# Moving the pool of converted weights and g by 64 bytes in a fused attention and MLP kernel

## The chip, the cores and the metric

The kernel runs on one core of one Trainium2 chip. The metric is the time of one execution in microseconds (us), and lower is better. Before the change the median of three runs is 1013.45 us (1012.03 to 1017.72).

## What is computed

Random-feature attention over 8 batches, 8 heads, 576 positions and a head size of 64, then an MLP with an ELU over the 4608 tokens of width 512, with 2048 hidden units:

```python
q_s, k_s = q * scale, k * scale                       # phi(x) = exp(h - max(h)) / sqrt(m),
q_p, k_p = phi(q_s), phi(k_s)                         # h = x @ omega.T - |x|^2 / 2
kv = einsum('bhsm,bhsd->bhmd', k_p, v); z = sum(k_p, axis=2)
attn = einsum('bhsm,bhmd->bhsd', q_p, kv) / (einsum('bhsm,bhm->bhs', q_p, z)[..., None] + 1e-06)
x = attn.transpose(0, 2, 1, 3).reshape(4608, 512)
h = x @ w_in                                          # 4608 x 2048
g = where(h > 0, h, exp(min(h, 0)) - 1)
out = g @ w_out                                       # 4608 x 512
```

## The kernel before

**Tiling.** The 4608 tokens are cut into 12 blocks of 384 (`TB`). The hidden units are cut into 16 slices of 128 (`NF`). One step of the MLP is one slice for one block, so there are 192 steps. The first three blocks are gone through twice with 8 slices each, the other nine once with 16 slices.

**Precision by halves.** Each MLP operand is held as a high part, in a reduced form that TensorE reads in one pass, and a low part that holds what is left. The weights of the first layer are `w1c` (high at `[:, 0]`, low at `[:, 1]`), the input is `xh` and `xl`, the second layer's weights are `w2h` and `w2l`, and the activation is `g` (high and low). Each product is three matmuls: high by high, high by low, low by high.

**Layer 1** (`layer1`, L1014 to L1016). For each of four chunks `c` of the width, three matmuls of 384 columns. The stationary operand, which is loaded into the array ahead of the matmul, is a 128x128 slice of `w1c`. The moving operand, which is streamed through, is `xh` or `xl`. That makes 12 matmuls a step, 2304 in all. Then ScalarE and VectorE make `g` from the result (L1023 to L1027, then the two halves of `g`).

**Layer 2** (`layer2`, L1052 to L1054). For each of three groups of 128 tokens, three matmuls of 512 columns: 9 a step, 1728 in all. The stationary operand is a 128x128 slice of `g`, and the moving operand is `w2h` (L1052, L1054) or `w2l` (L1053). While one matmul streams, TensorE loads the stationary operand of the next.

**Attention.** 32 pairs of heads are worked through beside the MLP. Their matmuls stand between those of the MLP: L566 (`om` streamed, `tk` or `tq` loaded), L776 (`zr` streamed, `ones` loaded), L732 (a transpose: `ident` streamed, a part `kvt` of a `zs` buffer loaded), and others. `visit` and `finish` hold these.

**Order.** A planner (`Plan`) gives each operation a due time and a cost and writes out the order of every engine ahead of time. It works from constants and does not look at addresses.

**Where things lie.** The bytes of a partition are given out in the order of the pools. The pool `const` comes first: `ident`, `ones`, `of`, `om`, two `kvf`, `w2h`, `w2l`, `xh`, `xl`. All of these have sizes that are multiples of 256 bytes, so they all start at the same place modulo 256. Then come the padding tile `gap0`, the pool `mv` (three `w1c` buffers of 4096 bytes, three `g` buffers of 3072 bytes) and the pool `sb`, which begins with the padding tile `gap1` and holds the rest. `sb` has, in this order, the tiles for loads (`xk`, `xq` and so on, 3 of 4608 bytes), the tiles `tk` and `tq` (2 of 4608), `v` (2, each taking 2624 bytes), two small ones of 512, the four buffers `raw` and `zs` (4608 apart), and then the smaller and later tiles.

The slices that the matmuls take move by multiples of 256 bytes too (512 bytes for a chunk of `w1c` or a token group of `g`, 1536 for a block of `xh`, 2048 for a slice of `w2h`). So each pair of a streamed and a loaded operand has one fixed distance modulo 256. The lines that set it:

```python
GAP = 48                                              # L33
    const.tile([P, GAP], F32, name="gap0")            # L391: 4 * GAP bytes
    sb.tile([P, 64 - GAP], F32, name="gap1")          # L392
```

Of the kernel before, what the change touches and what calls it, by code (L numbers as in the profile page):

```python
# [29 lines left out]
NTT = TB // P  # L30
NBLK = NTOK // TB
RING = 2 * S
GAP = 48  # L33
NJ = 9
NV = 10 * (D + 1)
SCALE = 1.0 / (float(D) ** 0.25)
# [303 lines left out]
def performer_elu_kernel(  # L340
# [49 lines left out]

    const.tile([P, GAP], F32, name="gap0")  # L391
    sb.tile([P, 64 - GAP], F32, name="gap1")  # L392

# [810 lines left out]
```

## Time and profile before

| | |
|---|---|
| median of three runs | 1013.45 us (1012.03, 1013.45, 1017.72) |
| profiled execution | 1011.99 us, span 1010.2 us |
| granted TensorE clock, mean | 0.999 |
| PE busy (matmul) | 995.6 us, 99% of the span, 5806 matmuls |
| PEld busy (weight load) | 883.0 us, 87% |
| DVE, ACT, POOL busy | 722.9, 656.2, 254.1 us (72%, 65%, 25%) |

Matmuls overlap in the pipeline and their ends are modelled, so the duration of one is longer than the distance between two starts. PE is TensorE's matmul, PEld its weight load, DVE is VectorE, ACT is ScalarE and POOL is GpSimd. A name such as `acc<-w2h,g` gives the output, the streamed operand and the loaded operand, in that order.

### The profile page before, as it was taken

What the parts mean: (1) busy time and instruction counts of PE and PEld (TensorE: products, weight loads), DVE (VectorE), ACT (ScalarE), POOL (GpSimd) and SP (SyncE); (2) the same over time, 40 slices, a digit from 0 to 9 for tenths busy, and PEclk for the clock granted to TensorE, in tenths of its full rate; (3) what the DMA queues carried; (4) which work ended last, traced back from release to release, by engine and by line L of the source; (5) the groups of instructions that cost most, each with busy time, mean ns of one, the idle gap of its engine ahead of it and who ended that gap; (6) DMA issues with size and microseconds to landing.
All of it is one profiled execution on the core that took longest, in us unless ns stands there. A gap on an engine that the chain in (4) does not pass through costs nothing. (4 is left out here: it accounts for less than half of the span.)

```text
span 1010.2 us, 18666 instructions
## 1 busy us (share of the span) xinstructions
PE 995.6 (99%) x5806; PEld 883.0 (87%) x5806; DVE 722.9 (72%) x2605; ACT 656.2 (65%) x1797; POOL 254.1 (25%) x273
## 2 busy tenths in 40 slices
PE   9899999999999999999999999999999999999998
PEld 8788889888888988999888988999888888899997
DVE  7999998559979974367888985448788886433332
ACT  7888744589869954268878983438888884322322
POOL 3666532333423320012322421003322241000000
PEclk9999999999999999999999999999999999999999
DMA  9577877467796875347666775435777644533431
GB/s 226 177 219 247 270 273 260 167 231 262 242 294 215 265 234 164 137 155 227 215 221 210 268 242 181 156 125 181 250 230 237 236 156 155 175 130 129 163 133 53
DMA packets 73779, 204.91 MB, mean 203 GB/s; under 512 B 10256, under 2 KB 22736, under 8 KB 73680
## 3 DMA queue, kind: packets, MB, share of 16 engines
q1 hardware_dynamic: 73680, 203.72, 61.7%
q8 instruction: 47, 0.77, 0.3%
q14 instruction: 52, 0.43, 0.1%
HBM read 169.35 MB, written 34.34 MB: 202 GB/s over the span
## 5 line engine op out<-in xcount | busy, mean ns | idle before, releaser
L1014 PE MATMUL ph<-xh,w1c 128*128 128x384 f32 x768 | 261.9, 341 | 1.0 <-DVE e L1027 1.0
L1015 PE MATMUL ph<-xl,w1c 128*128 128x384 f32 x768 | 258.3, 336 | 0.0
L1016 PE MATMUL ph<-xh,w1c 128*128 128x384 f32 x768 | 258.1, 336 | 0.0
L1023 ACT ACTIVATE e<-ph 128x384 f32<-128x384 f32 x192 | 95.0, 495 | 223.9 <-PE ph L1016 214.1
L1052 PE MATMUL acc<-w2h,g 128*128 128x512 f32 x576 | 228.1, 396 | 0.0
L1053 PE MATMUL acc<-w2l,g 128*128 128x512 f32 x576 | 227.0, 394 | 0.0
L1054 PE MATMUL acc<-w2h,g 128*128 128x512 f32 x576 | 224.6, 390 | 0.0
L1027 DVE SCALAR_TENSOR_TENSOR e<-e,ph 128x384 f32<-128x384 f32 x192 | 105.3, 550 | 164.3 <-ACT e L1024 162.9
L1014 PEld LDWEIGHTS ph<-xh,w1c 128*128 128x128 f32 x768 | 144.4, 188 | 19.9 <-DVE e L1027 2.3
L1015 PEld LDWEIGHTS ph<-xl,w1c 128*128 128x128 f32 x768 | 144.4, 188 | 12.9
L1016 PEld LDWEIGHTS ph<-xh,w1c 128*128 128x128 f32 x768 | 144.4, 188 | 0.0
L404 POOL TENSOR_TENSOR hq<-hq,den 128x512 f32<-128x512 f32 (+1 forms) x96 | 81.6, 862 | 228.0 <-DVE den L806 159.8
L1054 PEld LDWEIGHTS acc<-w2h,g 128*128 128x128 f32 x576 | 108.1, 188 | 24.3
L1052 PEld LDWEIGHTS acc<-w2h,g 128*128 128x128 f32 x576 | 108.3, 188 | 7.5 <-issue 1.3
L1053 PEld LDWEIGHTS acc<-w2l,g 128*128 128x128 f32 x576 | 108.3, 188 | 4.9 <-POOL w2l L404 0.3
L404 DVE TENSOR_TENSOR g<-e,g 128x384 fp32r<-128x384 f32 x176 | 103.6, 590 | 3.2
L1024 ACT ACTIVATE e<-e 128x384 f32<-128x384 f32 x192 | 101.5, 530 | 3.5
L659 POOL TENSOR_TENSOR zs<-hk 128x512 f32<-128x512 f32 x24 | 31.1, 1297 | 218.9 <-ACT hk L488 160.1
L797 DVE CUSTOM_DVE_ANT_0 junk<-hq,pz 128x128 f32<-128x128 f32 (+1 forms) x320 | 73.9, 279 | 6.5 <-PE pz L776 4.5
L575 ACT ACTIVATE p2k<-ppk,sqk 128x128 f32<-128x128 f32 x216 | 66.3, 369 | 18.4 <-PE ppk L566 12.1
L488 ACT ACTIVATE hk<-hk,mnk 128x128 f32<-128x128 f32 x216 | 68.9, 401 | 4.3 <-DVE mnk L584 4.2
L401 DVE CAST g<-e 128x384 fp32r<-128x384 f32 x168 | 64.5, 386 | 9.8 <-PE acc L1054 0.9
(184 smaller groups left out, 1472.8 us busy)
## 6 DMA issues: line engine op xcount, KB each, us to landing
w1c<-w1s SPq DMA_DIRECT2D x176, 512.0 KB, 3.5
raw_w<-in_w_dram SPq DMA_DIRECT2D x32, 512.0 KB, 4.9
xk<-in_kx_dram SPq DMA_DIRECT2D x24, 576.0 KB, 4.8
xq<-in_qx_dram SPq DMA_DIRECT2D x24, 576.0 KB, 4.4
turned<-tb SPq DMA_DIRECT2D x24, 576.0 KB, 3.0
qh<-turned SPq DMA_DIRECT2D x96, 144.0 KB, 4.8
v<-in_v_dram SPq DMA_DIRECT2D x32, 325.0 KB, 5.1
out_dram<-o SPq DMA_DIRECT2D x36, 256.0 KB, 4.1
```

The lines of the kernel that those rows point to most:

```text
L404: (nc.vector if e == "DVE" else nc.gpsimd).tensor_tensor(*args)
L488: nc.scalar.activation(h()[:, j, :], src(j), AF.Exp, bias=mn()[:, j:j + 1], scale=-1.0)
L797: nc.vector.tensor_tensor_reduce(out=junk()[r], in0=h()[r, j, :], in1=pz()[r, a * P:(a + 1) * P], scale=1.0, scalar=EPS, op0=ALU.mult, op1 ...
L1014: nc.tensor.matmul(ph(), wh, xh[:, c, o:o + TB], start=(c == 0), stop=False)
L1015: nc.tensor.matmul(ph(), wh, xl[:, c, o:o + TB], start=False, stop=False)
L1016: nc.tensor.matmul(ph(), wl, xh[:, c, o:o + TB], start=False, stop=(c == NC - 1))
L1023: op("ACT", act(TB, True), due, lambda: nc.scalar.activation(e(), ph(), AF.Relu, scale=-1.0), (p,), (e,))
L1024: op("ACT", act(TB), due + 0.2, lambda: nc.scalar.activation(e(), e(), AF.Exp, scale=-1.0), (e,), (e,))
L1027: lambda: nc.vector.scalar_tensor_tensor(e(), e(), -1.0, ph(), ALU.add, ALU.max), (p, e), (e,),
L1052: nc.tensor.matmul(a(), g()[:, 0, ts], w2h[:, f], start=(f == f0), stop=False)
L1053: nc.tensor.matmul(a(), g()[:, 0, ts], w2l[:, f], start=False, stop=False)
L1054: nc.tensor.matmul(a(), g()[:, 1, ts], w2h[:, f], start=False, stop=(f == f1 - 1))
```

## The change

One constant. `gap0` shrinks from 192 to 128 bytes and `gap1` grows from 64 to 128 bytes. So the pool `mv`, with all `w1c` and `g` buffers, begins 64 bytes lower. Nothing else moves, and no instruction is added, removed or put elsewhere.

```diff
-GAP = 48
+GAP = 32
```

Before, `mv` began 192 bytes past a place that has the streamed tiles' position modulo 256, which is the same as 64 bytes ahead of one. After, it begins 128 bytes past.

## The prediction

> **What bounds the kernel now.** I read the page's first part, then the chain that ended last, then the groups by line.
>
> ```profile
> span 1010.2 us, 18666 instructions
> ...
> PE 995.6 (99%) x5806; PEld 883.0 (87%) x5806; DVE 722.9 (72%) x2605; ACT 656.2 (65%) x1797; POOL 254.1 (25%) x273
> ...
> PE 19%; ACT 3%; DVE 1%; issue 0%; ACTq 0%
> PE acc L1053 3%; PE acc L1052 3%; PE acc L1054 3%; PE ph L1014 3%; PE ph L1015 3%; PE ph L1016 3%; PE pn L702 1%; ACT hq L488 1%; ACT p2q L575 1%; ACT hk L488 0%; ACT p2k L575 0%; ACT e L1024 0%; DVE hk L584 0%; PE _(28, 29)_(30, 31)_10802 L715 0%; DVE junk L797 0%
> ...
> L1014 PE MATMUL ph<-xh,w1c 128*128 128x384 f32 x768 | 261.9, 341 | 1.0 <-DVE e L1027 1.0
> ```
>
> TensorE is never idle for long: 1010.2 - 995.6 = 14.6 us in all. What a matmul costs, though, is not its duration but the distance to the next start. The timeline of PE in a stretch without attention shows it (start, duration):
>
> ```profile
> 940.91 0.39 PE L1052 MATMUL acc<-w2h,g 128*128 128x512 f32 x1
> 941.14 0.39 PE L1053 MATMUL acc<-w2l,g 128*128 128x512 f32 x1
> 941.37 0.39 PE L1054 MATMUL acc<-w2h,g 128*128 128x512 f32 x1
> 941.60 0.39 PE L1052 MATMUL acc<-w2h,g 128*128 128x512 f32 x1
> ...
> 942.29 0.34 PE L1014 MATMUL ph<-xh,w1c 128*128 128x384 f32 x1
> 942.46 0.34 PE L1015 MATMUL ph<-xl,w1c 128*128 128x384 f32 x1
> 942.63 0.34 PE L1016 MATMUL ph<-xh,w1c 128*128 128x384 f32 x1
> 942.81 0.34 PE L1014 MATMUL ph<-xh,w1c 128*128 128x384 f32 x1
> ```
>
> Three layer 1 matmuls take 942.81 - 942.29 = 0.52 us, 0.173 each; three of layer 2 take 941.60 - 940.91 = 0.69, 0.230 each. So a duration is the spacing plus about 0.163 us (0.336 against 0.173, 0.392 against 0.230), and a nanosecond more on a duration is one more on the path. Layer 1 has 2304 matmuls, 2304 x 0.173 = 399 us; layer 2 has 1728, 1728 x 0.230 = 397 us. Together 796 of 1010 us run at a pace that this change can touch. The views by source line give the pace finely (minimum, median and maximum of a duration in ns):
>
> ```profile
> L1015 PE MATMUL ph<-xl,w1c x768: 332/336/341, 41.2 to 998.5; 128*128 128x384 f32 x192
> ...
> L1016 PE MATMUL ph<-xh,w1c x768: 331/336/341, 41.3 to 998.7; 128*128 128x384 f32 x192
> ...
> L1052 PE MATMUL acc<-w2h,g x576: 387/392/505, 62.2 to 1005.7; 128*128 128x512 f32 x192
> ...
> L1053 PE MATMUL acc<-w2l,g x576: 387/394/501, 62.4 to 1006.0; 128*128 128x512 f32 x192
> ...
> L1054 PE MATMUL acc<-w2h,g x576: 388/388/418, 62.7 to 1006.2; 128*128 128x512 f32 x192
> ```
>
> The reader is to see steps. Layer 1 sits at 336 and has a floor of 331 to 332. L1054 sits on its floor of 388, L1052 and L1053 stand 4 and 6 above it. Two L1052 and L1054 matmuls stream the same slice of `w2h`, so something beside the streamed columns sets the pace.
>
> **Does the distance modulo 256 matter in this trace?** The change adds and removes no instruction. All it does is turn the distance of every MLP load from its stream from 192 (that is, -64) into 128. The trace has streams of `xh` and `w2h` during loads that lie elsewhere: those of attention. `ones` is in the same pool as the streams, and `tk` and `tq` lie at multiples of 256 from them (after `gap0`, `mv` and `gap1`: 192 + 64 bytes), distance 0. `kvt` lies 2048 bytes into a `zs` buffer, and between the start of `sb` and that buffer stand 5 tiles of 4608, two of 2624 and two of 512 bytes: distance 5248 modulo 256 = 128, the distance after the change. Groups by line in windows of a few ns give the durations; first the streams during loads of `tk`, `tq` or `ones` at distance 0 (L1016 at 205.5 and 835.9 us, the first and the last of 99; L1054 at 206.7 us, the first of 88, and at 765.9 us):
>
> ```profile
> L1016 PE MATMUL ph<-xh,w1c 128*128 128x384 f32 x1 | 0.3, 339 | 0.0
> ...
> L1016 PE MATMUL ph<-xh,w1c 128*128 128x384 f32 x1 | 0.3, 337 | 0.0
> ...
> L1054 PE MATMUL acc<-w2h,g 128*128 128x512 f32 x1 | 0.4, 393 | 0.0
> L1054 PE MATMUL acc<-w2h,g 128*128 128x512 f32 x1 | 0.4, 389 | 0.0
> ```
>
> The 99 have the median 339 and the mean 338.2; most of the 88 are at 389 or 393, mean 392.3. So with the load at distance 0 an `xh` stream costs 2 to 3 ns more than the 336 at -64, and a `w2h` stream 1 to 5 more than 388. The distance does seem to be felt. Now the loads of `kvt` at distance 128 (PEld, then the streams: L1016 at 246.4 and 845.8 us, the first and last of 13; L1054 at 324.8 and 846.6 us, the first and last of 6):
>
> ```profile
> 846.37 0.19 PEld L1054 LDWEIGHTS acc<-w2h,g 128*128 128x128 f32 x1
> 846.60 0.14 PEld L732 LDWEIGHTS pkt<-ident,zs 128*128 128x128 f32 x1
> ...
> L1016 PE MATMUL ph<-xh,w1c 128*128 128x384 f32 x1 | 0.3, 341 | 0.0
> L1016 PE MATMUL ph<-xh,w1c 128*128 128x384 f32 x1 | 0.3, 336 | 0.0
> ...
> L1054 PE MATMUL acc<-w2h,g 128*128 128x512 f32 x1 | 0.4, 393 | 0.0
> L1054 PE MATMUL acc<-w2h,g 128*128 128x512 f32 x1 | 0.4, 392 | 0.0
> ```
>
> The 13 run from 333 to 341, median 336, mean 336.7; all 6 are at 392 or 393. These loads differ in kind: they feed a transpose and show 0.14 us where the MLP's show 0.19, so they are a near row and not the same thing. For that reason I take no more than their direction.
>
> **The sum.** Layer 1, 2304 matmuls: the `kvt` rows give +0.7 ns, the rows at distance 0 up to +2.7. The `kvt` load is the shorter and may hide part of the cost, so I take the middle, +1.7: 2304 x 1.7 = 3.9 us (ends 1.6 and 6.2). On the other side nothing excludes the floor of 332, -4: -9.2 us. L1054, 576 matmuls: 388 to 392.7 by the six rows, 576 x 4.7 = 2.7 us; it cannot gain, since its median is its minimum. L1052 would go from 392 to the same 393, +0.6 us, and L1053 from 394 to 393, -0.6 (ends for the two: both at 388, -2.3 and -3.5; both 5 up, +5.8). The start covers a little, because there TensorE waits for others:
>
> ```profile
> core 0: us, PE busy (x) PEld busy (x) DVE busy (x) ACT busy (x) POOL busy (x), PEclk, DMA share, GB/s
> 0.00:50.00 50.00, 44.20 (x336) 40.19 (x336) 41.45 (x159) 40.21 (x120) 25.53 (x31) 1.00 0.75 202
> 50.00:100.00 50.00, 48.42 (x333) 42.81 (x330) 49.42 (x147) 41.65 (x115) 32.32 (x27) 1.00 0.73 231
> ...
> 600.00:700.00 100.00, 100.00 (x529) 89.95 (x529) 54.24 (x190) 47.90 (x125) 8.12 (x9) 1.00 0.50 166
> ...
> 0.00:100.00 100.00, 8.14 (x25) 4.76 (x25) 1.00 0.74 216
> ```
>
> VectorE has 49.42 of 50 us there, so the first two windows follow it; by the last row, that of L1015 alone, they hold 25 of 768 such matmuls, 3% of the sum, -0.2 us. From 100 us on nothing covers a slower stream, and a faster one would be kept until VectorE is late (54 of 100 us at 600, so there is room). The loads of `w1c` by DMA, the writes of `g` and the order keep their sizes and places in the queues; I cost them at nothing, since the chain above shows no DMA. Sum: 3.9 + 2.7 + 0.0 - 0.2 = +6.4 us. The profiled execution is 1011.99 us, 1.46 below the median; +6.4 gives 1018.4 against it and 1019.9 against the median. I forecast 1020.
>
> **A rule that speaks against it.** The Trainium skill, page "SBUF — State Buffer", section "Who interferes with whom", says that TensorE has one read port for the moving operand and an independent one for weight loads, and that "PE and ACT never wait on anyone." By it the position of a load could not change the pace of a stream, and the sum would be 0, 1013.45 us. The rows at distance 0 (339 beside 336) do not agree with it.
>
> **Rivals.** *Nothing happens.* The pace may depend on the neighbouring instruction's kind rather than its address: all rows off the usual pace are followed by attention. Or only distance 0 hurts, and -64 and 128 are alike: for it speaks the median of 336 in the 13 rows, against it the six at 392 and 393. Time: 1013.5. *Faster.* At 128 the load may avoid the stream for good, and layer 1 goes to its floor of 332: 2304 x 4 = 9.2 us, 1004. With L1052 and L1053 at 388 too it would be another 5.8, 998.5. For it speaks that the floor exists at all; against it that only few matmuls reach it at present and that none of the six rows of L1054 stays on its floor. It decides from 2.2 ns a layer 1 matmul (5.1 / 2304) if layer 2 stays. *Slower by more.* 128 may be as bad as 0: layer 1 at 339, 2304 x 3 = 6.9, and L1054 at 393, 2.9: +9.8, 1023; with L1052 up by 5 too (2.9) it is 1026.
>
> **How the numbers follow.** Half a per cent, 5 us, is about what a measurement of this kernel can tell from no change. Slower by more than that: 0.43 (my forecast 0.28, slower by more 0.15), with a range of its own from 1018.5 to 1026. Nothing, or too little to tell: 0.32. Faster: 0.25. The range from 1003 to 1026 takes in the floor of layer 1 on one side and the worst rows on the other, and leaves out about 2 in 10.
>
> **What would show it.** In the changed profile the medians by source line: L1014 to L1016 from 336 to 338, L1054 from 388 to 393, L1052 and L1053 at 393. The counts of all engines stay, and the busy times of DVE, ACT and POOL stay within their noise. The first 100 us should hardly move; 600 to 700 us should hold fewer matmuls than 529. Layer 1 at 332 or below would make the prediction wrong in sign; unchanged medians would mean the address is not felt at this distance, and that the rows at distance 0 show the kind of the neighbour.

## Result and profile after

The changed kernel takes 1020.04 us (median of 9 runs, 1017.52 to 1021.41) against 1013.73 us (9 runs) before. The ratio is 1.0063, with a 95% interval of 1.0049 to 1.0077: 6.4 us slower. The profiled executions lie further apart than the medians, since the one after is the slowest of its nine (1021.41 us) and the one before is faster than any of its nine (1011.99 us): their spans differ by 9.4 us. The sums over one execution below are to be held against this 9.4.

The page of the changed kernel, its span and first part (busy us, share, count):

```profile
span 1019.6 us, 18666 instructions
...
PE 1004.4 (99%) x5806; PEld 888.4 (87%) x5806; DVE 723.4 (71%) x2605; ACT 656.4 (64%) x1797; POOL 253.2 (25%) x273
```

Every engine has its count of before, and every engine but TensorE its busy time to within 0.9 us. The instructions of each engine stand in the same order. TensorE's idle time is 1019.6 - 1004.4 = 15.2 us, where it was 14.6, so hardly any idle time was added. The time is in the matmuls themselves. Groups by line, first after, then before (busy us and mean ns of one):

```profile
L1014 PE MATMUL ph<-xh,w1c 128*128 128x384 f32 x768 | 263.4, 343 | 0.8 <-DVE e L1027 0.8
L1016 PE MATMUL ph<-xh,w1c 128*128 128x384 f32 x768 | 260.1, 339 | 0.0
L1015 PE MATMUL ph<-xl,w1c 128*128 128x384 f32 x768 | 259.6, 338 | 0.0
...
L1052 PE MATMUL acc<-w2h,g 128*128 128x512 f32 x576 | 229.8, 399 | 0.0
L1054 PE MATMUL acc<-w2h,g 128*128 128x512 f32 x576 | 227.5, 395 | 0.0
L1053 PE MATMUL acc<-w2l,g 128*128 128x512 f32 x576 | 227.0, 394 | 0.0
```

```profile
L1015 PE MATMUL ph<-xl,w1c 128*128 128x384 f32 x768 | 258.3, 336 | 0.0
L1016 PE MATMUL ph<-xh,w1c 128*128 128x384 f32 x768 | 258.1, 336 | 0.0
L1052 PE MATMUL acc<-w2h,g 128*128 128x512 f32 x576 | 228.1, 396 | 0.0
L1053 PE MATMUL acc<-w2l,g 128*128 128x512 f32 x576 | 227.0, 394 | 0.0
L1054 PE MATMUL acc<-w2h,g 128*128 128x512 f32 x576 | 224.6, 390 | 0.0
```

With L1014 at 261.9 before, the differences are 1.5, 1.3 and 2.0 us for layer 1 and 1.7, 0.0 and 2.9 us for layer 2 (L1052, L1053, L1054). Together that is 9.4 us, as much as the spans differ by. Not all of it can be put down to the distance. The first layer 1 matmul of step 7 starts at 99.66 us before and at 100.95 after, so 1.3 us were lost with only 6 of the 192 steps run, and 0.8 of the 4.8 us of layer 1 lie there. TensorE's clock differed from 47.5 to 52.5 us (the third number from the end of a row, 0.66 and 1.00, is the share of the full clock that was granted; first after, then before):

```profile
47.50:52.50 5.00, 5.00 (x25) 3.63 (x25) 4.63 (x9) 3.00 (x7) 2.01 (x2) 0.66 0.83 285
...
47.50:52.50 5.00, 4.99 (x34) 3.84 (x32) 5.00 (x8) 2.60 (x7) 2.39 (x2) 1.00 0.86 283
```

The maxima of 522 ns in the next view are from there. The lower clock does not belong to the new distance: a later run, with the streams and the loads both moved and the distance as before, has such a stretch too (0.51 from 47.5 to 50 us). How much of the 1.3 us comes from it is not shown.

The views by source line of the changed kernel (minimum, median, maximum in ns), against 336, 336, 392, 394 and 388 before:

```profile
L1015 PE MATMUL ph<-xl,w1c x768: 331/337/522, 40.7 to 1007.8; 128*128 128x384 f32 x192
...
L1016 PE MATMUL ph<-xh,w1c x768: 330/338/522, 40.9 to 1008.0; 128*128 128x384 f32 x192
...
L1052 PE MATMUL acc<-w2h,g x576: 387/394/506, 63.1 to 1015.2; 128*128 128x512 f32 x192
...
L1053 PE MATMUL acc<-w2l,g x576: 387/393/502, 63.3 to 1015.4; 128*128 128x512 f32 x192
...
L1054 PE MATMUL acc<-w2h,g x576: 388/394/405, 63.6 to 1015.6; 128*128 128x512 f32 x192
```

L1054 has left its floor: before, median and minimum were both 388. Where attention is over (from 871 us on before), the pace shows undisturbed. Groups by line of the changed kernel from 900 to 1000 us; before, the same window has the means 336, 336, 336, 392, 388, 394:

```profile
L1016 PE MATMUL ph<-xh,w1c 128*128 128x384 f32 x96 | 32.5, 338 | 0.0
L1015 PE MATMUL ph<-xl,w1c 128*128 128x384 f32 x96 | 32.4, 338 | 0.0
L1014 PE MATMUL ph<-xh,w1c 128*128 128x384 f32 x96 | 32.4, 337 | 0.0
L1052 PE MATMUL acc<-w2h,g 128*128 128x512 f32 x71 | 28.2, 397 | 0.0
L1054 PE MATMUL acc<-w2h,g 128*128 128x512 f32 x71 | 28.0, 395 | 0.0
L1053 PE MATMUL acc<-w2l,g 128*128 128x512 f32 x71 | 28.0, 394 | 0.0
```

A step of the MLP has four matmuls of each layer 1 line and three of each layer 2 line, so by the durations it is 4 x (2 + 2 + 1) + 3 x (5 + 7 + 0) = 56 ns longer there. The starts, which are not modelled as the ends are, give the exact figure. These are the first matmuls of the steps 162 and 192, before and then after:

```profile
873.97 0.34 PE L1014 MATMUL ph<-xh,w1c 128*128 128x384 f32 x1
...
996.11 0.34 PE L1014 MATMUL ph<-xh,w1c 128*128 128x384 f32 x1
...
881.35 0.35 PE L1014 MATMUL ph<-xh,w1c 128*128 128x384 f32 x1
...
1005.38 0.34 PE L1014 MATMUL ph<-xh,w1c 128*128 128x384 f32 x1
```

The lag grows from 7.38 to 9.27 us over 30 steps, 63 ns a step. From step 7 to step 162, with attention in between, it grows from 1.29 to 7.38 us, only 39 ns a step.

### The profile page after: what moved, and what is told of

It is laid out like the page before. It is cut to its first block, busy times and chain, and to the rows that moved or that the text cites. A ratio compares the mean times of both kernels' runs of the same rounds, so it can differ in the third digit from the quotient of the medians.

```text
span 1019.6 us, 18666 instructions
## 1 busy us (share of the span) xinstructions
PE 1004.4 (99%) x5806; PEld 888.4 (87%) x5806; DVE 723.4 (71%) x2605; ACT 656.4 (64%) x1797; POOL 253.2 (25%) x273
## 4 chain that ended last, share of the span: by engine, by line
PE 85%; ACT 5%; DVE 5%; DMA 4%; issue 1%; SPq 0%; POOL 0%; ACTq 0%; DVEq 0%
PE acc L1052 12%; PE ph L1014 12%; PE acc L1054 12%; PE acc L1053 12%; PE ph L1016 12%; PE ph L1015 12%; PE ppq L566 2%; PE pn L702 2%; PE ppk L566 2%; DMA w1c<-w1s 1%; DMA xk<-in_kx_dram 1%; PE ppk L516 1%; ACT hk L488 1%; ACT hq L488 1%; PE pkv L621 1%
## 5 line engine op out<-in xcount | busy, mean ns | idle before, releaser
L1014 PE MATMUL ph<-xh,w1c 128*128 128x384 f32 x768 | 263.4, 343 | 0.8 <-DVE e L1027 0.8
L1016 PE MATMUL ph<-xh,w1c 128*128 128x384 f32 x768 | 260.1, 339 | 0.0
L1015 PE MATMUL ph<-xl,w1c 128*128 128x384 f32 x768 | 259.6, 338 | 0.0
L1052 PE MATMUL acc<-w2h,g 128*128 128x512 f32 x576 | 229.8, 399 | 0.0
L1054 PE MATMUL acc<-w2h,g 128*128 128x512 f32 x576 | 227.5, 395 | 0.0
L1053 PE MATMUL acc<-w2l,g 128*128 128x512 f32 x576 | 227.0, 394 | 0.0
L1014 PEld LDWEIGHTS ph<-xh,w1c 128*128 128x128 f32 x768 | 144.7, 188 | 19.3 <-issue 1.9
L1015 PEld LDWEIGHTS ph<-xl,w1c 128*128 128x128 f32 x768 | 144.8, 189 | 14.9
L1016 PEld LDWEIGHTS ph<-xh,w1c 128*128 128x128 f32 x768 | 144.5, 188 | 0.0
L1054 PEld LDWEIGHTS acc<-w2h,g 128*128 128x128 f32 x576 | 108.3, 188 | 25.8
L1052 PEld LDWEIGHTS acc<-w2h,g 128*128 128x128 f32 x576 | 108.3, 188 | 7.3 <-issue 1.3
L1053 PEld LDWEIGHTS acc<-w2l,g 128*128 128x128 f32 x576 | 108.6, 189 | 5.7 <-POOL w2l L404 0.3
```

Of the source, the lines that this page charges most:

```text
L1014: nc.tensor.matmul(ph(), wh, xh[:, c, o:o + TB], start=(c == 0), stop=False)
L1015: nc.tensor.matmul(ph(), wh, xl[:, c, o:o + TB], start=False, stop=False)
L1016: nc.tensor.matmul(ph(), wl, xh[:, c, o:o + TB], start=False, stop=(c == NC - 1))
L1052: nc.tensor.matmul(a(), g()[:, 0, ts], w2h[:, f], start=(f == f0), stop=False)
L1053: nc.tensor.matmul(a(), g()[:, 0, ts], w2l[:, f], start=False, stop=False)
L1054: nc.tensor.matmul(a(), g()[:, 1, ts], w2h[:, f], start=False, stop=(f == f1 - 1))
```

## Experiments

The theory: the pace of a matmul depends on the distance modulo 256 between what it streams and the operand that is loaded beside it. The main rival: the absolute place of `w1c` and `g` counts, because VectorE, ScalarE and the DMAs write them there. Ratios are to the kernel before on the same chip, with 95% intervals.

**Streams moved, loads left alone.** `w2h`, `w2l`, `xh` and `xl` go up by 64 bytes, and `w1c` and `g` keep every address of before.

```diff
+    const.tile([P, 16], F32, name="gapc")
     w2h = const.tile([P, NF, DM], F32R, name="w2h")
-GAP = 48
+GAP = 32
-    sb.tile([P, 64 - GAP], F32, name="gap1")
+    sb.tile([P, 48 - GAP], F32, name="gap1")
```

> w1c and g lie exactly where they lay before; w2h, w2l, xh and xl are 64 bytes higher, so the distance is 128 as after the change. Theory (distance): as the changed kernel, 1.005 to 1.008 of before, medians 337 to 338 in layer 1 and 394 in L1054. Rival (the absolute place of w1c and g matters, for the engines and DMAs that write them): 1.000, within 0.002.

Measured: 1018.73 us, 1.0059 (1.0045 to 1.0072), as the change. By source line (all lines one further down, since a line was added; L1055 is L1054 of before):

```profile
L1016 PE MATMUL ph<-xl,w1c x768: 331/337/343, 41.6 to 1005.1; 128*128 128x384 f32 x192
...
L1055 PE MATMUL acc<-w2h,g x576: 388/394/417, 63.1 to 1012.9; 128*128 128x512 f32 x192
```

Nothing was moved under the engines and DMAs that write `w1c` and `g`, and the slowdown is there in full. The distances of attention's tiles from the moved streams change too, in this run and the next, but those tiles are loaded beside few streams, and the next run is as fast as the kernel before.

**Both moved.** `w1c` and `g` are 64 bytes higher too, distance -64.

```diff
+    const.tile([P, 16], F32, name="gapc")
     w2h = const.tile([P, NF, DM], F32R, name="w2h")
-    sb.tile([P, 64 - GAP], F32, name="gap1")
```

> Streamed tiles and w1c and g all 64 bytes higher, distance -64 as before. Theory (distance): 1.000 of before, within 0.002, with 336 and 388 as medians. Rival (absolute place): a time of its own, off by 0.003 or more, and equal to that of the kernel with distance 0, in which w1c and g have these same addresses.

Measured: 1013.14 us, 1.0006 (0.9997 to 1.0015). The medians are those of before:

```profile
L1015 PE MATMUL ph<-xl,w1c x768: 332/336/522, 41.0 to 999.9; 128*128 128x384 f32 x192
...
L1054 PE MATMUL acc<-w2h,g x576: 388/388/400, 63.0 to 1007.5; 128*128 128x512 f32 x192
```

**Distance 0.** `w1c` and `g` as in the run before this one, the streams as in the kernel before.

```diff
-GAP = 48
+GAP = 64
-    sb.tile([P, 64 - GAP], F32, name="gap1")
```

> w1c and g 64 bytes higher than before, streams as before, distance 0. Theory (distance): slower than before as attention's loads at distance 0 suggest, layer 1 at 339 and L1054 at 392 to 393: +3 x 2304 + 4.5 x 576 = 9.5 us, 1.009. Rival (absolute place): equal to the kernel with both moved up. Second rival (the slow rows beside attention came from the kind of the neighbour, not from distance 0): 1.000.

Measured: 1017.94 us, 1.0049 (1.0036 to 1.0061). It has the same `w1c` and `g` addresses as the run with both moved, and is 0.4% slower. Those three and the kernel before make a square: two places of the streams, two of the loads. Both kernels at -64 are fast, and both others are slow; the main rival falls. Distance 0 costs 5.0 us, half of the 9.5 expected. By source line and by group (one line further up; L1013 is L1014 of before, L1015 is L1016), the last row from 900 to 1000 us alone:

```profile
L1015 PE MATMUL ph<-xh,w1c x768: 333/334/346, 41.8 to 1003.2; 128*128 128x384 f32 x192
...
L1015 PE MATMUL ph<-xh,w1c 128*128 128x384 f32 x768 | 259.2, 338 | 0.0
...
L1013 PE MATMUL ph<-xh,w1c 128*128 128x384 f32 x96 | 32.1, 334 | 0.0
```

The median of L1016 of before, 334, would make it faster at 0 than at -64 (336), but its mean is 338: about half take 334 and many of the others 339 to 346, so a median alone misleads here. L1014 of before is faster in the undisturbed window (334 against 336). The rows beside attention had given 339 for that distance.

**One part alone.** First `w1c` at 128 with `g` left at its address, then the reverse. `g` gets a pool of its own with a pad ahead of it.

```diff
+    mg = ctx.enter_context(tc.tile_pool(name="mg", bufs=1))
-        g = gt[F] = Buf(mv, [P, 2, TB], F32R, "g", f"g_{F}", 3)
+        g = gt[F] = Buf(mg, [P, 2, TB], F32R, "g", f"g_{F}", 3)
+    mg.tile([P, 16], F32, name="gap2")     # w1c alone, with GAP = 32, gap1 16 floats
+    mg.tile([P, 48], F32, name="gap2")     # g alone, with GAP = 48, gap1 32 floats
```

> Only w1c lies 64 bytes lower (distance 128); g stays where it was (192). Theory (each load slows the stream that it runs beside): the streams of L1014 and L1015 and those of L1016 and L1054 with w1c behind them slow down, 2.2 ns for some 1811 of layer 1 and 5.5 ns for some 337 of layer 2, 5.8 us, 1.0045 to 1.006; L1052 and L1053 stay at 392 and 394. Rival (a single one of the two layers carries it, layer 2): 1.000 to 1.002.

> Only g is moved, to distance 128; w1c stays at 192 (the tiles of the pool behind move by 256 bytes, which changes no distance). Theory: the streams with g behind them slow down: L1052 by 3.6 ns x 576, L1054 by 6 x 121, L1016 by 2.4 x 356, L1053 by 0.2, together 3.8 us, 1.003 to 1.005; L1014 and L1015 stay at 336. With the run that moves w1c alone this adds up to the change, 1.006 to 1.008. Rival (layer 2 carries all): 1.006 to 1.008 here.

Measured: `w1c` alone 1019.37 us, 1.0063 (1.0049 to 1.0077); `g` alone 1016.00 us, 1.0027 (1.0019 to 1.0036). The rival that layer 2 carries all falls. `w1c` alone cost a little more than expected (1.0045 to 1.006), `g` alone a little less (1.003 to 1.005), and their intervals reach into these ranges. But the parts do not add up: 6.4 and 2.7 make 9.1 us, and the change costs 6.4. By source line, `w1c` alone, then `g` alone (two lines further down; L1016 is L1014 of before):

```profile
L1016 PE MATMUL ph<-xh,w1c x768: 331/339/667, 41.8 to 1007.1; 128*128 128x384 f32 x192
...
L1016 PE MATMUL ph<-xh,w1c x768: 332/338/668, 40.4 to 1002.3; 128*128 128x384 f32 x192
```

With `w1c` alone at 128, the median of L1014 of before is 339, more than in the changed kernel (337). With `g` alone moved it is 338, though it streams beside a load of `w1c`, whose place did not change. So a matmul's pace also depends on the pairs ahead of it.

**Distance 64.**

```diff
-GAP = 48
+GAP = 16
```

> The whole pool 128 bytes lower than before: distance 64. By the run with streams and loads alone, layer 1 at 64 took 173.3 ns a matmul as at 192, layer 2 took 233.2 against 229.2. Theory (distance; layer 1 alike, layer 2 slower by 4): 1728 x 4 = 6.9 us, 1.004 to 1.008. Rival (64 on either side of the stream is the same): 1.000.

Measured: 1017.78 us, 1.0043 (1.0029 to 1.0056). As the theory had it, 64 on the other side of the stream is not the same as -64. The cost is 4.4 us, where 6.9 were expected.

**Streams and loads alone.** A kernel that only streams one tile, again and again, beside loads at a set distance; no other engine works then.

```python
for e in range(40):      # for n = 384 (a) and 512 (b), o = distance / 4
    nc.tensor.matmul(p[:, 0:n], w[:, o:o + 128], s[:, 0:n], start=(e == 0), stop=(e == 39))
```

> This kernel leaves the whole computation out: it streams one tile through TensorE again and again while the load of the next matmul reads another tile at a set distance, 0 to 256 bytes in steps of 16, then 320 and 448; 40 matmuls of 384 columns (a) and 40 of 512 (b) for each, with no other engine at work. Theory (distance between stream and load modulo 256): durations differ by distance, repeat at 256, 320 (as 64) and 448 (as 192); 384 columns: 336 ns at 192, 337 to 338 at 128, 339 at 0; 512 columns: 388 to 392 at 192, 393 to 394 at 128. Rival (the address alone costs nothing, other engines' accesses to the moved tiles do): one duration for all distances, within 1 ns.

Measured, groups by line, the names giving columns and distance:

```profile
L68 PE MATMUL b128x<-s,w 128*128 128x512 f32 x40 | 9.5, 395 | 0.0
...
L68 PE MATMUL b192x<-s,w 128*128 128x512 f32 x40 | 9.3, 392 | 0.0
...
L68 PE MATMUL a128x<-s,w 128*128 128x384 f32 x40 | 7.2, 338 | 0.0
...
L68 PE MATMUL a192x<-s,w 128*128 128x384 f32 x40 | 7.1, 336 | 0.0
```

The paces of the kernel are here with TensorE alone: 336 and 392 at 192, 338 and 395 at 128. From start to start that is 173.3 and 176.1 ns for 384 columns, 229.2 and 233.4 for 512. Two expectations failed: distance 0 is no slower than 192 (173.3 for 384 columns; for 512 it is faster, 227.6), and with 384 columns 320 (176.7) is not as 64 (173.3).

**Steps alone.** The matmuls of a whole MLP step (12 and 9), one or both distances varied. They come in threes, of one layer and the other by turns, with six of layer 1 where two steps meet. That is not quite the kernel's order: where attention is over, its trace has 3 of layer 1, 6 of layer 2, 9 of layer 1 and 3 of layer 2 to a step.

```python
steps(192, d, f"{d:03d}g", 6)     # g alone at d        (w1c distance, g distance, name, steps)
steps(d, 192, f"{d:03d}w", 6)     # w1c alone at d
steps(d, d, f"{d:03d}z", 6)       # both at d;  d = 0, 16, ..., 240
```

> This kernel leaves the whole computation out except the order of the MLP's matmuls: steps of 12 matmuls of layer 1's kind and 9 of layer 2's kind, on tiles that never change, with no other engine at work. w1c's distance (w), g's (g) or both (z) go from 0 to 240 bytes in steps of 16, the other one staying at 192; 6 steps each. Theory (distance, and the array's two readers alone): at 192 a layer 1 matmul takes 173.3 ns from start to start, at 128 it takes 175 to 177; a layer 2 matmul averages 229 at 192 and 232 to 235 at 128, as in the changed kernel, where the three lines average 237, 232 and 233. Rival (the slower pace at 128 in the kernel comes from other engines in between): 128 and 192 alike within 1 ns a matmul.

Measured, as 12 times the mean distance of starts in layer 1 plus 9 times that in layer 2, beside what the kernel with the same distances lost:

```
both at      192     128     0       64      w1c at 128   g at 128   (ns a step, TensorE alone)
             4141    4201    4207    4193    4210         4160
more x 192   -       11.6    12.8    10.0    13.2         3.7        us
kernel       -       6.4     5.0     4.4     6.4          2.7        us, from the ratios
```

```profile
L76 PE MATMUL a128w<-xh,w1c 128*128 128x384 f32 x48 | 15.4, 339 | 0.0
L76 PE MATMUL a128z<-xh,w1c 128*128 128x384 f32 x48 | 15.4, 338 | 0.0
...
L76 PE MATMUL a192z<-xh,w1c 128*128 128x384 f32 x48 | 15.3, 336 | 0.0
L76 PE MATMUL a128g<-xh,w1c 128*128 128x384 f32 x48 | 15.2, 334 | 0.0
```

TensorE alone shows that the parts do not add: `w1c` alone costs 69 ns a step, `g` alone 19, both 60. Of all 48 settings none is below 4140, and only 192 for both (4140) and `g` at 240 (4140.5) reach it.

The kernels lose less by their times than this run has it for 192 steps. The starts in their traces show where the difference lies. This is what a step loses against the kernel before, in ns, from step 7 to 162 (attention in between) and from 162 to 192 (attention over):

```
both at               128   128 (streams moved)   0    64   w1c at 128   g at 128   192 (both moved)
steps 7 to 162        39    27                    19   12   33           16         6
steps 162 to 192      63    63                    39   45   66           26         0
steps alone           60    60                    66   52   69           19         -
```

Where attention is over, the kernel loses about what TensorE alone loses, but for distance 0 (39 against 66). Since the order of the matmuls differs between the two, the price of a distance may depend on that order; no run tries it alone. Beside attention every changed distance loses less. That attention breaks up the pattern of the steps would explain it; it is not shown. One execution stands behind each column, and the last column, with the distance of before, shows that 6 ns can be chance in the first row.

**Period and history.** Both distances over 256 and beyond, three times in different orders; then the second layer's tiles shifted against the first's, with each load at 192 from its own stream.

> As the run with steps alone, no other engine at work and the rest of the computation left out. First, both distances together at 192, 448, 704, 128, 384, 64, 320, 0 and 256, all three times in different orders (u, v, w). If only the distance modulo 256 counts: 448 and 704 give the 4140 ns a step of 192, 384 gives the 4201 of 128, 320 the 4193 of 64, 256 the 4207 of 0, each within 10 ns and the same in all three orders. Rival (a longer period, or a state carried over from the matmuls before): 448 or 384 off by more than 15 ns, or the same distance off by that much between the orders. Second (s), the second layer's streams and g both shifted by 0 to 240 bytes against the first layer's tiles, each load staying at 192 from its own stream: what remains are the matmuls at the seams between the layers, one in seven. Theory: within 4140 and 4190, none below 4125, so no placement is left that beats the kernel before by a measurable amount.

In this run every matmul took 3.57 times as long, at any distance (a step 14780 ns), so it says nothing on the question. The same kernel once more:

> The kernel of the run before this one once more, since in that run every matmul, whatever its distance, took 3.57 times as long (a step 14780 ns), so that it says nothing on distances. Expected now: steps of 4140 to 4220 ns. If only the distance modulo 256 counts: 448 and 704 give the 4140 ns of 192, 384 the 4201 of 128, 320 the 4193 of 64, 256 the 4207 of 0, within 10 ns, the same in all three orders. Rival (a longer period, or a state carried over): off by more than 15 ns between these or between orders. With the second layer's tiles shifted against the first's (s): within 4140 and 4190, none below 4125.

Measured in the second run:

```
distance     192    448    704    128    384    64     320    0      256
order u      4140   4140   4140   4200   4200   4195   4193   4209   4207   ns a step
order v      4140   4140   4139   4200   4202   4193   4194   4205   4207
order w      4140   4140   4140   4200   4200   4195   4195   4208   4208
```

```profile
L80 PE MATMUL a128u<-xh,w1c 128*128 128x384 f32 x48 | 15.4, 338 | 0.0
...
L80 PE MATMUL a384u<-xh,w1c 128*128 128x384 f32 x48 | 15.4, 337 | 0.0
...
L80 PE MATMUL a192u<-xh,w1c 128*128 128x384 f32 x48 | 15.3, 336 | 0.0
L80 PE MATMUL a448u<-xh,w1c 128*128 128x384 f32 x48 | 15.3, 336 | 0.0
```

In these steps the distance modulo 256 is all that counts, to within 5 ns in 4200, whatever ran before. That 64 and 320 differed in the simpler run did not come back here. The shifts between the layers' tiles gave 4140 to 4220, none lower; one of them, by 80 bytes, took 4220 where at most 4190 was expected. So nothing tried beats the kernel before, as far as steps in this order tell.

**Smaller loads.** The simpler kernel with loads of 128, 96, 64 and 32 columns (`w[:, o:o + m]` into `p[0:m, 0:n]`).

> As the first run of streams and loads alone (40 matmuls of 384 columns, a, and of 512, b), the rest left out, but the load beside each stream has 128, 96, 64 or 32 columns (l128 to l032), at distances 192, 128, 64 and 0. Theory (the load's reads delay the stream's while both run): the time from start to start falls with the columns of the load and the distances draw together; at 32 columns a 384 stream takes some 164 to 167 ns at every distance and a 512 stream 217 to 220. Rival (the 13 ns over a smooth stream are a fixed cost of changing the stationary operand, and only the spread comes from distance): 170 ns or more at 32 columns.

```profile
L68 PE MATMUL a192l032x<-s,w 128*32 128x384 f32 x40 | 7.2, 338 | 0.0
...
L68 PE MATMUL a192l128x<-s,w 128*128 128x384 f32 x40 | 7.1, 336 | 0.0
```

The theory of this run fails. A load of 32 columns takes 108 ns in the trace where one of 128 takes 188, yet it leaves the stream no faster (384 columns: 175.5 ns from start to start at 192, 173.3 to 175.0 at the others; 512 columns: 230.6 to 231.7). The order of the distances changes too: with 384 columns 192 is the slowest. So it is not shown that the load's reads hold up the stream's for as long as both run. That the pace follows the distance is shown; the mechanism behind it stays open.

## Why the prediction was right

**The bound.** That a nanosecond on an MLP matmul is one on the path held closely: the six groups grew by 9.4 us, the span by 9.4, and TensorE's idle time by 0.6. It is not exact: where attention is over, the durations give 56 ns a step and the starts 63.

**That the distance is felt.** Right, and it is the step on which the sign hung. The square of four kernels shows it apart from the absolute place. The rival that nothing happens does not hold: with no other engine at work, 128 costs 176.1 ns where 192 costs 173.3. The Trainium skill, page "SBUF — State Buffer", section "Who interferes with whom", says that PE never waits on anyone. Taken as the prediction took it, that the place of a load cannot change the pace of a stream, these runs do not agree with it (176.1 beside 173.3 ns). What in TensorE or its reads makes the difference is open.

**Layer 1, +1.7 ns a matmul, 3.9 us.** By the groups +1.7 to +2.6 ns (1.5, 1.3 and 2.0 us over 768): 4.8 us in these two executions, and 3.9 without the first six steps. Right in size. **L1054, +4.7 ns, 2.7 us:** 2.9 us. **L1052, +1 ns, 0.6 us:** the median went up by 2, the group by 1.7 us, more than forecast, as its mean of 397 in the quiet stretch shows, where it had 392. **L1053, -1 ns:** the median went from 394 to 393 as forecast, the group stayed at 227.0.

**Where it was right with a weaker reason than it seemed.** The price was read from streams beside `kvt`, at distance 128. Their distance did not change, yet their durations did. Here are the first and last of them in the changed kernel (L1016 at 248.4 and 852.9 us, L1054 at 327.1 and 853.6):

```profile
L1016 PE MATMUL ph<-xh,w1c 128*128 128x384 f32 x1 | 0.3, 338 | 0.0
...
L1016 PE MATMUL ph<-xh,w1c 128*128 128x384 f32 x1 | 0.3, 341 | 0.0
...
L1054 PE MATMUL acc<-w2h,g 128*128 128x512 f32 x1 | 0.4, 395 | 0.0
L1054 PE MATMUL acc<-w2h,g 128*128 128x512 f32 x1 | 0.4, 392 | 0.0
```

The 13 L1016 have the mean 339.5 where they had 336.7, at the same distance as before. The 99 at distance 0, which did not change either, went from 338.2 to 337.5. A single pair amid another pattern does not have the price of a pattern of such pairs. The rows at distance 0 show it more sharply: taken as a price they gave 9.5 us for a kernel at distance 0, which lost 5.0. The caution of taking only a direction from these rows, and the middle of their ends for layer 1, kept the forecast near. That it came out at +6.4 us, to the tenth the 6.4 us of the ratio, is luck: the prices came from rows that do not give the price, the L1052 term was a third of what the two traces show, and these two executions differ by 9.4.

**The DMAs, costed at nothing.** The reason given was that the chain showed no DMA, but the shares of that chain (19, 3 and 1%) make up under a quarter of the span; it reaches back no further than 768 us. The chain of the changed kernel covers the whole span and has some:

```profile
PE 85%; ACT 5%; DVE 5%; DMA 4%; issue 1%; SPq 0%; POOL 0%; ACTq 0%; DVEq 0%
```

Nothing in the runs says that the DMAs' share changed with the distance, but the reason was weaker than it looked.

**Signs to look for.** Medians of 338 for layer 1 (measured 337 to 338), 393 for L1054 (394) and 393 for L1052 and L1053 (394, 393) came. That the first 100 us would hardly move held only in part: 1.3 of the 9.4 us were lost there, in an execution with a stretch of lower clock. That 600 to 700 us would hold fewer matmuls than 529 did not come; in the changed kernel that window has

```profile
600.00:700.00 100.00, 100.00 (x551) 89.16 (x548) 52.26 (x164) 46.33 (x117) 8.03 (x10) 1.00 0.53 170
```

because other work, with shorter matmuls, has moved into it. A window fixed in time compares different work as soon as the kernel drifts. Of the rivals, "faster" does not occur in any kernel here, and no setting of the steps alone beat 192. One stream repeated can be faster, though: 512 columns take 227.6 ns at distance 0 and 229.2 at 192.

## What to carry to other kernels

When TensorE is busy all the time, compare the durations of the same matmul line between kernels to the nanosecond: a change of 0 to 5 ns on each of 4032 matmuls was nearly the whole result, with hardly any idle time to show for it. Compare means as well as medians, and the starts of matching matmuls in a stretch that nothing else disturbs. The distance modulo 256 bytes between streamed and loaded tiles is a thing to set and to sweep, in the kernel itself or in the order in which its matmuls run, since neither a single stream repeated nor a chance pair in a trace gives its price. To tell a relative cause from an absolute one, move the other partner.

## What was not expected of the hardware

The distances do not follow a simple rule such as "far is good": with steps alone, 192 costs 4140 ns, while 128, 64 and 0 cost 4200, 4193 and 4207. The parts of a step do not add up either (69 and 19 ns apart, 60 together). A stream of 384 columns takes 173 to 176 ns from start to start beside a load of 32 columns just as beside one of 128.

One execution ran mostly at 629 ns from start to start of a layer 1 matmul, instead of 173, 3880.89 us in all, and the same kernel took 1106.06 us the next time, on another chip. The kernel before took 1013.22 us on the chip of the slow execution. The clock is given as 1.00 for both, but the traces of these two executions hold no record of the clock, so the cause is open.
